# Delta rule and two-level mixture of experts on one core: loads and stores asked for in transfers by rows

## The chip, the core and the metric

The kernel runs on one core of a Trainium2 chip. The core has a matrix engine (TensorE, in the profile PE, its weight loads PEld), a vector engine (VectorE, DVE), a scalar engine (ScalarE, ACT), GpSimd (POOL) and SyncE (SP), which issues most of the DMAs; sixteen DMA engines move the bytes. The metric is the time of one execution on the device in microseconds (us). A difference is called faster or slower here when it is over 2%; smaller ones count as the same.

## The reference

The first half is a delta rule with a state per batch and head, B=4, H=8, S=768 tokens, D=48; the second sends each of the 3072 tokens to one of 16 experts, group first, then expert in the group.

```python
k_n = k / (np.linalg.norm(k, axis=-1, keepdims=True) + 1e-06)
for t in range(S):
    y[:, :, t] = einsum('bhd,bhde->bhe', q[:, :, t], state)
    v_old = einsum('bhde,bhd->bhe', state, k_n[:, :, t])
    state = state + beta_t * einsum('bhd,bhe->bhde', k_n[:, :, t], v[:, :, t] - v_old)
x = y.transpose(0, 2, 1, 3).reshape(3072, 384)
g_idx = argmax(x @ w_group);  e_idx = argmax(xg @ w_expert[g])        # one expert for a token
out[tok] = g_w * e_w * (np.maximum(x_tok @ w1[g, e], 0) @ w2[g, e])   # 384 -> 1024 -> 384
```

All is float32.

## The kernel before

**The recursion** works on 24 chunks u of 32 tokens, all four batches and eight heads at once. For each chunk there are two loads. `load_kq(u)` brings keys and queries as columns: 112 rows (48 rows of the even heads, 16 of padding, 48 of the odd heads) of 1024 numbers; with a second argument it brings one half (a = 0 the keys, a = 1 the queries), 112 rows of 512. `load_kv(u)` brings keys and values as rows, 128 of 832 numbers. Twelve buffers (`NB`) hold the first kind, three (`NV`) the second. `load_con(0)` and `load_con(1)` bring the constants in two parts, the second with the identity matrix.

`gram(u)` multiplies a chunk's keys with its keys and queries (L258 for the first two chunks, L273); `inverse(g)` builds for four chunks at once, by many small VectorE instructions (L313 to L416, most of them L382 and L388), the inverse that replaces the steps inside a chunk, and `spread` puts it into `mtb` (L425 on VectorE, L427 on ScalarE). `scale(u)` multiplies the chunk's values with a norm (`vh`, L463, VectorE); it is the first reader of `kv`. `advance(u)` is the step of the chain: the products with the state (L486, L495), with the inverse (L503), the update of the state (L514, which reads the keys in `kv`), the output (L528), and copies by ScalarE between them. `logits(u)` and `route(r)` choose experts and sort tokens while the recursion goes on.

**The prologue** runs the products of chunks 0 to 9 before the recursion's first step. The SP queue gets the loads in bursts: `begin(bursts[i])` puts, ahead of each load, a ScalarE copy of one column into the tile that is to be filled (L800), so the load waits in SP's queue until ScalarE has come past the products before it. All five engines run in the order in which the program is written, so an instruction that waits holds what stands behind it on its engine. Before the first L503 stand, on TensorE, the products of chunks 8 and 9 and four products that clear the state's memory (L834).

**In step u of the recursion** the program issues at the end `load_kq(u + 12)` (until chunk 23 is asked for), `load_kv(u + 3)`, the store of the chunk's output `x` to `x_dram` (L990), and from u = 12 on one of the `pieces` of the weights of the first expert: first six with two transfers of 32 rows each of its `w1` (L151), then four of its `w2` (L158). `scale(u + 2)` stands in the first half of step u, so `load_kv(u + 3)`, which has to wait until L514 has read the buffer, is wanted in the first half of the step behind it. SP's other work, the loads of later experts (L167 to L174) and the transfers of results (L1171 to L1176), comes behind the recursion.

**The experts** follow from about 220 us on: for each a load of 3 MB of weights, a gather of its tokens, two products (L1112, L1131), and a scatter.

## Time and profile before

| | before |
|---|---|
| time, median of 3 runs | 494.39 us (488.39 to 496.58) |
| profiled execution: time | 493.09 us |
| profiled execution: span | 491.1 us |
| busy PE / DVE / ACT / POOL | 450.0 / 240.6 / 192.8 / 176.8 us |
| mean rate of all DMAs | 198 GB/s |

The profile is one execution. Its span is the time from the program's first to its last instruction; 2.0 us of the time lie outside it. In rows of the timeline, the first two numbers are the start and the length in us, `SPq` is SP issuing a transfer (its length is that of the issue, not of the transfer), and brackets tell how long the engine stood idle before the instruction and what ended that. In the chain (work followed back from the end to what released it) a row `DMA` has the issue of a transfer and the time until its landing released the next. A table by windows has for each stretch the busy time of each engine with the count of instructions, then the TensorE clock granted, the mean share of the 16 DMA engines that was busy, and their rate in GB/s.

### The profile page before, as it was taken

How to read it: one execution, taken by the hardware profiler on the slowest of the kernel's cores; microseconds unless marked ns; L12 is line 12 of the kernel's file. 1: busy time of each engine (PE TensorE's matmuls, PEld its weight loads, DVE VectorE, ACT ScalarE, POOL GpSimd, SP SyncE). 2: the span in 40 equal slices, each digit the busy share in tenths (PEclk: the TensorE clock that was granted, in tenths of full speed). 3: DMA queues.
4: the chain of work that ended last, by engine and by line, in shares of the span. 5: the costliest groups of instructions: out<-in, count | busy, mean ns of one | idle time of the engine just before them, and what ended most of it. 6: DMA issues, size and time to landing. Idle time of an engine off the chain costs nothing.

```text
span 491.1 us, 18102 instructions
## 1 busy us (share of the span) xinstructions
PE 450.0 (92%) x7730; PEld 425.9 (87%) x7730; DVE 240.6 (49%) x872; ACT 192.8 (39%) x413; POOL 176.8 (36%) x300
## 2 busy tenths in 40 slices
PE   3338999999999999999999999999999999999992
PEld 3335888888888888789999999999999999999992
DVE  4988998997999998565201201220122112201110
ACT  3335579688897976541112111111211111111120
POOL 0031310415416400103456355544745456255131
PEclk9999599899999999999999999999999999999997
DMA  5566344455434455307977877858997789778820
GB/s 163 149 186 200 100 150 153 128 151 174 144 109 123 145 161 166 90 23 177 370 238 229 277 254 208 300 186 274 318 298 228 255 302 322 248 215 273 308 80 27
DMA packets 56757, 97.07 MB, mean 198 GB/s; under 512 B 18974, under 2 KB 41433, under 8 KB 56675
## 3 DMA queue, kind: packets, MB, share of 16 engines
q1 hardware_dynamic: 50755, 85.89, 54.6%
q0 software_dynamic: 5920, 10.00, 6.5%
q8 instruction: 62, 1.02, 0.9%
q14 instruction: 20, 0.16, 0.1%
HBM read 81.75 MB, written 14.27 MB: 196 GB/s over the span
## 4 chain that ended last, share of the span: by engine, by line
PE 55%; DMA 12%; issue 11%; ACT 7%; DVE 7%; POOL 7%; SPq 0%; POOLq 0%; DVEq 0%
PE y_ps L1131 16%; PE h_ps L1112 16%; DMA out_dram<-yo,to_i 7%; POOL xq L1084 5%; DMA kqt<-in_kq_dram 4%; PE w_ps L503 4%; PE s_ps L514 3%; ACT s_bd L520 3%; PE a_ps L486 2%; PE o_ps L528 2%; PE o_ps L495 2%; DVE m L388 2%; DVE below L382 2%; PE t_ps L554 2%; PE l_ps L456 1%
## 5 line engine op out<-in xcount | busy, mean ns | idle before, releaser
L1131 PE MATMUL y_ps<-hid,w 128*128 128x224 f32 (+15 forms) x768 | 132.2, 332 | 0.0
L1131 PEld LDWEIGHTS y_ps<-hid,w 128*128 128x128 f32 x768 | 129.1, 190 | 0.3
L1112 PE MATMUL h_ps<-xt,w 128*128 128x232 f32 (+14 forms) x720 | 122.7, 330 | 0.0
L1112 PEld LDWEIGHTS h_ps<-xt,w 128*128 128x128 f32 x720 | 120.1, 190 | 0.3
L1084 POOL DMA_INDIRECT xq<-x_dram,from_q x92 | 87.6, 952 | 35.0 <-issue 24.1
L1134 DVE COPY yt<-y_ps 128x232 f32<-128x232 f32 (+13 forms) x14 | 5.1, 365 | 144.4 <-PE y_ps L1131 144.4
L1115 ACT ACTIVATE hid<-h_ps 128x448 f32<-128x448 f32 (+15 forms) x64 | 32.1, 501 | 100.2 <-PE h_ps L1112 98.2
L1143 POOL DMA_INDIRECT out_dram<-yo,to_i x32 | 34.1, 1065 | 93.2 <-DVE yo L1181 83.7
L1136 ACT ACTIVATE yt<-y_ps 128x224 f32<-128x224 f32 (+15 forms) x34 | 11.4, 336 | 116.6 <-PE y_ps L1131 116.6
L382 DVE TENSOR_TENSOR below<-m 128x16 f32<-128x16 f32 (+4 forms) x180 | 53.3, 299 | 0.2
L388 DVE TENSOR_TENSOR m<-m,below 128x16 f32<-128x16 f32 (+4 forms) x180 | 53.0, 295 | 0.4
L520 ACT ACTIVATE s_bd<-s_ps 48x768 f32<-48x768 f32 x46 | 37.0, 804 | 5.6 <-PE s_ps L514 5.1
L1181 DVE TENSOR_SCALAR yo<-yr,gate 128x384 f32<-128x384 f32 (+14 forms) x28 | 11.1, 420 | 39.8 <-DMA yr<-y_dram 31.4
L503 PEld LDWEIGHTS w_ps<-f,mtb 64*64 64x64 f32 x736 | 24.6, 141 | 6.0 <-ACT f L490 3.9
L503 PE MATMUL w_ps<-f,mtb 64*64 64x48 f32 x736 | 27.5, 227 | 1.4 <-ACT f L490 1.4
L427 ACT ACTIVATE mtb<-mt,con 128x256 f32<-128x256 f32 x39 | 28.0, 741 | 0.0
L514 PE MATMUL s_ps<-w,kv 32*112 32x96 f32 x736 | 25.3, 273 | 0.9 <-ACT found L871 0.3
L514 PEld LDWEIGHTS s_ps<-w,kv 32*112 32x112 f32 x736 | 21.3, 178 | 3.8 <-ACT w L507 1.5
L528 PE MATMUL o_ps<-w,gqm 64*64 64x48 f32 x576 | 21.4, 225 | 2.5 <-issue 2.3
L486 PE MATMUL a_ps<-s_bd,kqt 112*32 112x96 f32 x736 | 21.1, 257 | 1.1 <-ACT s_bd L520 1.1
L495 PE MATMUL o_ps<-s_bd,kqt 112*32 112x96 f32 x736 | 21.8, 259 | 0.2 <-issue 0.2
L528 PEld LDWEIGHTS o_ps<-w,gqm 64*64 64x64 f32 x576 | 19.1, 139 | 3.3 <-issue 2.5
(184 smaller groups left out, 543.8 us busy)
## 6 DMA issues: line engine op xcount, KB each, us to landing
w<-in_w_dram SPq DMA_DIRECT2D x29, 1536.0 KB, 10.7
kv<-in_kv_dram SPq DMA_DIRECT2D x24, 416.0 KB, 3.2
kqt<-in_kq_dram SPq DMA_DIRECT2D x20, 448.0 KB, 4.8
x_dram<-x SPq DMA_DIRECT2D x24, 192.0 KB, 2.2
w<-in_w_dram SPq DMA_DIRECT2D x24, 128.0 KB, 3.8
y_dram<-yq SPq DMA_DIRECT2D x36, 84.0 KB, 9.4
yr<-y_dram SPq DMA_DIRECT2D x14, 192.0 KB, 2.5
kqt<-in_kq_dram SPq DMA_DIRECT2D x8, 224.0 KB, 3.6
```

The costliest lines, as they stand in the source:

```text
L382: nc.vector.tensor_tensor(t, column.to_broadcast(like), row.to_broadcast(like), op=ALU.mult)
L388: nc.vector.tensor_tensor(to, to, t, op=ALU.add)
L495: nc.tensor.matmul(o_ps[quads[b], 2 * j:2 * j + 2, :], lhsT=kqt[0:KR, 1, j, quads[b]], rhs=s_bd[0:KR, b, j], start=(j == 0), stop=False, s ...
L503: nc.tensor.matmul(w_ps[b, h], lhsT=mt[b, uu * H + (h % 2) * NP + h // 2], rhs=f[b, h], start=(h == 0), stop=True, skip_group_check=True)
L514: nc.tensor.matmul(s_at[0:KR, b, j], lhsT=k[quads[b], j, 0:KR], rhs=w[quads[b], 2 * j:2 * j + 2], start=(u == 0 and j == 0), stop=True, sk ...
L520: nc.scalar.activation(s_bd[rows, :, :, hh, :], s_at[rows, :, :, hh * D:(hh + 1) * D], ACT.Copy)
L528: nc.tensor.matmul(o_ps[b, h], lhsT=gq[b, hq].rearrange("p a t -> p (a t)"), rhs=w[b, h], start=(u == 0 and h == 0), stop=True, skip_group ...
L1084: nc.gpsimd.indirect_dma_start(out=xq[:, g, :], out_offset=None, in_=x_dram[:, :].rearrange("n (q c) -> (n q) c", q=4), in_offset=bass.Ind ...
L1112: nc.tensor.matmul(h_ps[:, k], lhsT=w1[:, j, (f + k) * 128:(f + k + 1) * 128], rhs=xt[:, j, 0:R], start=(j == 0), stop=(j == DC - 1), skip ...
L1115: nc.scalar.activation(hid[:, f:f + 2], h_ps, ACT.Relu)
L1131: nc.tensor.matmul(y_ps, lhsT=w2[:, f, j * 128:(j + 1) * 128], rhs=hid[:, f], start=(f == 0), stop=(f == FC - 1))
L1143: put = nc.gpsimd.indirect_dma_start(out=out[:, :], out_offset=bass.IndirectOffsetOnAxis(ap=to[0:P, i:i + 1], axis=0), in_=yo[0:P, :], in_ ...
```

## The change

A helper `by_rows` issues one transfer for each range of rows. Whole loads of keys and queries are cut into rows 0 to 31, 32 to 63 and 64 to 111; the loads of one half stay whole. Loads of keys and values, the second part of the constants and each of the four pieces of the first expert's `w2` become four transfers of 32 rows, and the store of `x` two of 64.

```diff
+    def by_rows(out, in_, cuts):
+
+        for a, b in zip(cuts, cuts[1:]):
+            nc.sync.dma_start(out=out[a:b], in_=in_[a:b])
+
+    quarters_of = range(0, 129, 32)
...
-            out.append(lambda a=a, b=b: nc.sync.dma_start(out=w2[:, a:b], in_=d[:, a:b]))
+            out.append(lambda a=a, b=b: by_rows(w2[:, a:b], d[:, a:b], quarters_of))
...
         def load_kq(u, a=None):
+            cuts = (0, 32, 64, KR) if a is None else (0, KR)
             half = slice(0, 2) if a is None else slice(a, a + 1)
-            nc.sync.dma_start(out=kqt_[u % NB][0:KR, half],
-                              in_=kq_d[u].rearrange("p (a j t) -> p a j t", a=2, j=NP)[:, half])
+            by_rows(kqt_[u % NB][0:KR, half],
+                    kq_d[u].rearrange("p (a j t) -> p a j t", a=2, j=NP)[:, half], cuts)

         def load_kv(u):
-            nc.sync.dma_start(out=kv_[u % NV], in_=kv_d[u])
+            by_rows(kv_[u % NV], kv_d[u], quarters_of)
...
-            nc.sync.dma_start(out=con[:, part], in_=const_d[:, part])
+            by_rows(con[:, part], const_d[:, part], quarters_of if i else (0, 128))
...
-                    nc.sync.dma_start(out=x_dram[1 + u * 128:1 + (u + 1) * 128], in_=xs[u])
+                    by_rows(x_dram[1 + u * 128:1 + (u + 1) * 128], xs[u], (0, 64, 128))
```

The order of the computing instructions is the same on PE, DVE, ACT and POOL; SP has 439 rows instead of 288, and waits for loads become waits for their parts. Three places show it.

SP, in the prologue: the burst behind the products of chunk 0 and the one behind it (kv_117 and kv_118 are the buffers of chunks 0 and 1, con is the second part of the constants, kqt_113 and kqt_114 are for chunks 8 and 9). Before:

```order
L204 DMA kv_117<-in_kv_dram 128x832 [waits DMAHW0_49,Activation_49]
L210 DMA con<-in_const_dram 128x753 [waits DMAHW1_49]
L204 DMA kv_118<-in_kv_dram 128x832 [waits DMAHW2_49]
L200 DMA kqt_113<-in_kq_dram 112x1024 [waits DMAHW3_49,Activation_49]
L200 DMA kqt_114<-in_kq_dram 112x1024 [waits DMAHW4_49,Activation_49]
```

After, its last ten of 18:

```order
L145 DMA kv_118<-in_kv_dram 32x832 [waits DMAHW0_49]
L145 DMA kv_118<-in_kv_dram 32x832 [waits DMAHW1_49]
L145 DMA kv_118<-in_kv_dram 32x832 [waits DMAHW2_49]
L145 DMA kv_118<-in_kv_dram 32x832 [waits DMAHW3_49]
L145 DMA kqt_113<-in_kq_dram 32x1024 [waits DMAHW4_49,Activation_49]
L145 DMA kqt_113<-in_kq_dram 32x1024 [waits DMAHW5_49]
L145 DMA kqt_113<-in_kq_dram 48x1024 [waits DMAHW6_49]
L145 DMA kqt_114<-in_kq_dram 32x1024 [waits DMAHW7_49,Activation_49]
L145 DMA kqt_114<-in_kq_dram 32x1024 [waits DMAHW0_49]
L145 DMA kqt_114<-in_kq_dram 48x1024 [waits DMAHW1_49]
```

Twelve issues instead of three now stand ahead of the loads for chunks 8 and 9, and the last of these wait for parts of the same burst: the transfer eight places ahead is a part of con or of kv_118.

SP, one step of the recursion (x is the chunk's output). Before:

```order
L200 DMA kqt_110<-in_kq_dram 112x1024 [waits DMAHW7_49,PE_49]
L204 DMA kv_119<-in_kv_dram 128x832 [waits DMAHW0_49,DVE_49,PE_49]
L990 DMA x_dram<-x_1941 128x384 [waits DMAHW1_49,Activation_49]
L200 DMA kqt_111<-in_kq_dram 112x1024 [waits DMAHW2_49,PE_49]
L204 DMA kv_117<-in_kv_dram 128x832 [waits DMAHW3_49,DVE_49,PE_49]
```

After:

```order
L145 DMA kqt_110<-in_kq_dram 32x1024 [waits DMAHW1_49,PE_49]
L145 DMA kqt_110<-in_kq_dram 32x1024 [waits DMAHW2_49]
L145 DMA kqt_110<-in_kq_dram 48x1024 [waits DMAHW3_49]
L145 DMA kv_119<-in_kv_dram 32x832 [waits DMAHW4_49,DVE_49,PE_49]
L145 DMA kv_119<-in_kv_dram 32x832 [waits DMAHW5_49,PE_49]
L145 DMA kv_119<-in_kv_dram 32x832 [waits DMAHW6_49,PE_49]
L145 DMA kv_119<-in_kv_dram 32x832 [waits DMAHW7_49,PE_49]
L145 DMA x_dram<-x_1999 64x384 [waits DMAHW0_49,Activation_49]
L145 DMA x_dram<-x_1999 64x384 [waits DMAHW1_49]
```

A step has nine transfers on SP instead of three, one more than there are counters, so the second half of x waits for the first part of the same step's kqt.

PE, a step of the recursion at chunk 4 (g_ps is the product of a later chunk's keys and queries, s_ps the state's update). Before:

```order
L273 MATMUL g_ps_1491<-kqt_106 32x64 [waits DMAHW3_49,Activation_49]
L273 MATMUL g_ps_1491<-kqt_106 32x64 x31
L514 MATMUL s_ps<-w_1487,kv_117 112x96 [waits DMAHW1_49,Activation_49]
L514 MATMUL s_ps<-w_1487,kv_117 112x96 x15
L456 MATMUL l_ps_1545<-wr,xt_1450 128x20 [waits PE_49,Activation_49]
```

After:

```order
L281 MATMUL g_ps_1537<-kqt_106 32x64 [waits DMAHW6_49,DMAHW5_49,Activation_49]
L281 MATMUL g_ps_1537<-kqt_106 32x64 [waits DMAHW7_49]
L281 MATMUL g_ps_1537<-kqt_106 32x64 x30
L522 MATMUL s_ps<-w_1533,kv_117 112x96 [waits Activation_49]
L522 MATMUL s_ps<-w_1533,kv_117 112x96 [waits DMAHW0_49]
L522 MATMUL s_ps<-w_1533,kv_117 112x96 [waits DMAHW1_49]
L522 MATMUL s_ps<-w_1533,kv_117 112x96 [waits DMAHW2_49]
L522 MATMUL s_ps<-w_1533,kv_117 112x96 x12
```

One wait for a load has become three or four, at the first products that read its rows; the second product of a g_ps already needs the last rows (the odd heads). VectorE's `vh` likewise waits for four counters instead of one.

## Prediction

> **What bounds the kernel now.** I read the table by windows first, to see which stretch a slower or faster load can touch.

> ```profile
> core 0: us, PE busy (x) PEld busy (x) DVE busy (x) ACT busy (x) POOL busy (x), PEclk, DMA share, GB/s
> 29.00:31.00 2.00, 0.00 (x0) 0.00 (x0) 2.00 (x7) 1.35 (x2) 0.00 (x0) 1.00 1.01 332
> 31.00:33.00 2.00, 0.00 (x0) 0.00 (x0) 2.00 (x7) 0.00 (x0) 1.69 (x7) 1.00 1.02 236
> 46.00:140.00 94.00, 90.59 (x2822) 80.31 (x2826) 87.50 (x348) 75.33 (x148) 25.86 (x82) 0.91 0.44 136
> 220.00:456.00 236.00, 236.00 (x1387) 235.35 (x1387) 42.62 (x87) 39.11 (x87) 117.63 (x132) 1.00 0.80 259
> 225.40:227.40 2.00, 2.00 (x13) 2.00 (x12) 1.50 (x8) 0.27 (x2) 1.57 (x2) 1.00 0.99 254
> ```

> From 220 us on TensorE is busy all of 236 us, and none of those transfers is edited: nearly half of the span cannot move. Between 46 and 140 us, most of the recursion, the DMA engines are busy 44% of the time; VectorE has 87.50 of 94 us of work, TensorE 90.59. There a load matters by when it lands, not by its bytes. Only the first 46 us have stretches where TensorE does nothing while the DMA engines are full (29 to 33 us). So I took the chain next, up to 41 us and around the one place behind that where it passes through a load.

> ```profile
> 6.79 4.30 DMA kqt<-in_kq_dram
> ...
> 13.40 4.67 DMA kqt<-in_kq_dram
> ...
> 20.39 2.58 DMA kqt<-in_kq_dram
> ...
> 28.30 6.21 DMA kqt<-in_kq_dram
> ...
> 35.81 1.09 PE g_ps L273 x59
> 36.89 2.86 PE s_ps L834 x4
> 39.76 1.64 PE w_ps L503 x32
> ...
> 78.79 3.96 DMA kv<-in_kv_dram
> 82.84 0.56 DVE vh L463
> ```

> Four loads of keys stand in the chain ahead of the first L503 at 39.76; the third (halves) is not cut by the change. The other three, 15.18 us, are what it can shorten or lengthen, and 78.79 is the one load of `kv` in the recursion that the chain goes through. The list of waits says how much VectorE lost to loads at all: two waits.

> ```profile
> DVE vh L463 <- DMA kv<-in_kv_dram: 3.7, 2, 2.3
> ```

> **The most that the prologue can give.** Behind the loads a second chain ends almost as late: the first inverse on VectorE.

> ```profile
> 28.29 0.56 DVE L463 TENSOR_TENSOR vh<-kv,normt 128x384 f32<-128x384 f32 x1 [1.43 <-DMA kv<-in_kv_dram]
> 36.18 0.47 DVE L425 TENSOR_SCALAR mtb<-mt,con 128x256 f32<-128x256 f32 x1
> 37.83 0.72 ACT L427 ACTIVATE mtb<-mt,con 128x256 f32<-128x256 f32 x1
> ```

> L425 ends at 36.65 and L427 takes 0.72, so L503 could start at 37.37 at the earliest: 39.76 - 37.37 = 2.39 us is the cap, and 3.82 if VectorE's own 1.43 us of waiting for the first `kv` went too.

> **Part 1, loads of the prologue.** What a part costs is its issue and its landing.

> ```profile
> 1.69 1.36 SPq L200 DMA_DIRECT2D kqt<-in_kq_dram  x3
> ...
> 24.56 0.35 SPq L204 DMA_DIRECT2D kv<-in_kv_dram  x1
> 24.95 1.21 SPq L210 DMA_DIRECT2D con<-in_const_dram  x1
> 26.22 0.42 SPq L204 DMA_DIRECT2D kv<-in_kv_dram  x1
> ...
> 167.40 2.31 SPq L151 DMA_DIRECT2D w<-in_w_dram  x2
> ```

> Three issues in 1.36 us are 0.45 us apart; two of 32 rows in 2.31 us show that it can be 1.16 each. No part of 96 to 192 KB of a load was seen alone; the nearest rows are L151, 32 rows and 128 KB, and the store of 192 KB, L990. The views by line tell their landings, and that of a whole `kv`, in the order L151, L990, L204:

> ```profile
> DMA to landing us min/median/max: 2.7/3.8/3.8
> DMA to landing us min/median/max: 1.8/2.2/3.2
> DMA to landing us min/median/max: 3.1/3.2/4.3
> ```

> At 13.40 the first load of the pair now ends with its third part, asked for at 13.40 + 2 x 0.45 = 14.30, landed 2.7 to 3.8 us later, at 17.0 to 18.1; before it was 18.07. I take 17.6, a gain of **0.5**. At 6.79 the same sum gives 10.4 to 11.5 against 11.09: **0**. For the pair at 28.30 SP is the question. Before, SP was done with what stands ahead at 26.64; now twelve issues from 24.56 on end at 24.56 + 12 x 0.45 = 29.96, 1.66 us behind the old 28.30. The first load's third part then goes at 30.86 and lands at 33.6 to 34.7; before, 28.30 + 6.21 = 34.51. The old landing was late since the engines were full (1.01 and 1.02 in 29 to 33 us) with the same bytes that they get now. I take 33.9, a gain of **0.6**; the bounds are a gain of 0.9 and a loss of 0.2. The two gains add up along the chain to 1.1, below the cap. They are hidden if L427 moves later by over 1.3 us (39.76 - 1.1 - 37.37).

> The first `kv` has its last part asked for at 24.56 + 1.35 = 25.91; by L990's landing it is there at 27.7 to 29.1, by L151's at 28.6 to 29.7, before just ahead of 28.29. I take 28.5, a loss of **0.2** on VectorE, which carries it into the stretch to 140 us. The constants of the second part are first read by TensorE at 36.89 (L834) and cost nothing: even two microseconds more are covered.

> **Part 2, the recursion.** `load_kq` is asked for twelve chunks ahead: nothing. `load_kv` is short of time only where VectorE is the bound.

> ```profile
> 71.32 0.33 SPq L204 DMA_DIRECT2D kv<-in_kv_dram  x1
> ...
> 74.87 0.56 DVE L463 TENSOR_TENSOR vh<-kv,normt 128x384 f32<-128x384 f32 x1
> ```

> There the load of 71.32 landed at about 74.5 (median 3.2) and had 0.3 us to spare; the one of 78.79 came 2.30 us late. With four parts the last is asked for 1.35 us later and is smaller than any row: landing 1.35 + 1.8 = 3.15 to 1.35 + 2.7 = 4.05 us after the first issue, against 3.2. I take 3.5, so 0.3 late at 82.84 and covered at 74.87: a loss of **0.3**, bounds a gain of 0.05 and a loss of 1.35 (0.85 at 82.84, 0.5 at 74.87). SP itself has room: nine issues of 0.45 are 4.1 us of a step of 7.47 (71.32 to 78.79), and the parts of one step come up when PE or ACT lets them.

> Stores of `x` in halves and `w2` in parts have no reader within 4 us: `x_dram` is read by gathers at the end of the recursion, the first expert's `w2` behind 220 us. They cost nothing as long as SP isn't late by a step.

> Added waits: three more on VectorE before each `vh`, one more on ScalarE before `x`, four or five on TensorE a step.

> ```profile
> L463 DVEq EVENT_SEMAPHORE  x15: 21/21/21, 42.2 to 190.2; - x15
> ```

> One takes 21 ns, and fifteen of them stood ahead of `vh`, while VectorE waited there for loads at two places only: the others were passed under the instruction before. I take **0**; if none were hidden, 8 x 24 x 0.021 = 4.0 us over all engines, of which perhaps half in the chain.

> **Sum.** -0.5 + 0 - 0.6 + 0.2 + 0.3 = -0.6 us. The profiled execution's time is 493.09, its span 491.1; so 492.5. The median of the runs shown is 1.3 us above the profiled one and the runs lie 8.2 us apart, so this is no change that can be measured: under 2% (9.9 us) I call it the same.

> **A rule against the change.** The row that bears on it stands above: in 225.4 to 227.4 us, with parts of 32 rows of the second expert's `w1` in flight beside a gather, the engines were 99% busy at 254 GB/s; in 29 to 31 us, with whole loads, 101% at 332. So parts of 32 rows may move at 254/332 = 0.77 of the rate. *Rival A* is that:

> ```profile
> kv<-in_kv_dram SPq DMA_DIRECT2D x24, 416.0 KB, 3.2
> kqt<-in_kq_dram SPq DMA_DIRECT2D x20, 448.0 KB, 4.8
> ```

> By these sizes a `kv`, 0.426 MB, takes 1.68 us instead of 1.28, so it lands 0.4 later still, and the first load of a pair, 0.459 MB, 1.81 instead of 1.38. Three pairs by 0.4 and two tight `kv` by 0.4 are 2.0, with the sum 494.5. Against it speaks 31 to 33 us, 236 GB/s with whole loads of 112 rows. [...]

> **Rival B, slower: the counters.** With eight counters a part waits for the part eight places ahead. Parts 0.45 us apart hold SP up once they need over 8 x 0.45 = 3.6 us to land. In the burst of 24.56, 18 parts would go in 2.25 rounds; at the 6.21 us of the row of 28.30 that is 14.0, so the last lands at 38.5 instead of 35.8 (the second product starts at 35.81), 2.7 us later than before. Loads of `kv` that meet a slow issue (1.16 instead of 0.45 us) are 2.1 us later; two such at tight places and the 0.3 make 4.5. In all 493.1 + 2.7 + 4.5 = **500.3**. For it speaks that the issue of con took 1.21 us; against it that a whole load in the recursion lands in 3.2, a part hardly above 3.6.

> **Rival C, faster: parts land earlier everywhere.** If parts spread evenly over the engines and the first ones start sooner, the prologue gives its cap of 3.82 and the `kv` of 78.79 its 2.30: 493.1 - 6.1 = **487.0**. The chain's long landings, 6.21 against 4.30 for the same bytes, show that there is room; against it, 2.30 us at that place come from a load that was asked for late (78.79, by L514), and parts cannot be asked for sooner.

> **That it does nothing** is the forecast's near neighbour, 493.1, and inside its own range.

> **How the numbers follow.** Forecast with its own range 490.5 to 494.0: 0.47. Rival A, 494.5: 0.18. B, 500.3: 0.13. C, 487.0: 0.18. Something else: 0.04. The range goes from C to short of B's time, with the loss of 2 to 4 us from waits that aren't hidden inside: 487 to 500. Over 2% against 494.39 is below 484.5 or above 504.3; no case lies there. For tails of C and of B and the rest I leave 0.03 and 0.04; within 2%, 0.93.

> **What would show it.** Right: the pair of 28.30 still asked for by SP at about 30 us, its first load landed at 33.5 to 34.7, first L503 near 38.7; `vh` waiting for loads in total 3 to 5 us; 220 us and behind shifted as a whole, with the same length. Part 1 is wrong if TensorE's waits for `kqt` don't fall or SP's issues in the prologue lie over 0.5 us apart; part 2 if `vh` waits at more than three places; the waits were not free if TensorE's step grows where no load is late. The forecast is off most if a clock below 1.00 (0.91 on the mean of 46 to 140 us) falls elsewhere in the changed run, since that moves TensorE by more than all terms here.

## The result, and the profile after

| | before | after |
|---|---|---|
| median, on one chip, 22 runs each | 492.31 us (487.98 to 498.48) | 494.24 us (490.82 to 499.2) |
| profiled execution: time / span | 493.09 / 491.1 us | 495.46 / 493.7 us |
| ratio after to before | | 1.0071, 95% interval 1.0047 to 1.0095 |

The change makes the kernel slower by 0.7%, 3.5 us. That is under the 2% that counts as a difference here, but the interval leaves no doubt of its sign, and the forecast had the other sign: 0.6 us faster. (Ratios compare undisturbed runs alone, so they can differ a little from the ratio of two medians.)

The table by windows shows where the DMA engines lost work. The rows answer to those of before: PE, PEld, DVE, ACT and POOL busy, the clock, the engines' share and GB/s.

```profile
29.00:31.00 2.00, 0.00 (x0) 0.00 (x0) 1.72 (x3) 1.65 (x3) 0.00 (x0) 1.00 0.73 198
31.00:33.00 2.00, 0.00 (x0) 0.00 (x0) 2.00 (x9) 0.00 (x0) 0.70 (x2) 1.00 0.61 177
33.00:35.00 2.00, 0.00 (x0) 0.00 (x0) 1.86 (x5) 0.00 (x0) 1.78 (x9) 1.00 1.01 272
46.00:140.00 94.00, 88.81 (x2874) 78.28 (x2873) 91.28 (x372) 77.34 (x151) 32.35 (x82) 0.96 0.53 145
220.00:456.00 236.00, 235.81 (x1439) 234.47 (x1438) 44.59 (x96) 39.26 (x88) 117.58 (x132) 1.00 0.81 260
```

From 220 us on nothing changed: TensorE is busy 235.81 of 236 us, before 236.00. The loss is ahead of that. In 29 to 33 us, where whole loads kept the engines 101% and 102% busy, they are now 73% and 61% busy, and from 30.9 to 31.8 us only 35%, at 87 GB/s. I read that as too little having been asked for; the chain says who did not ask. A row `SPq L145` is one issue of a part.

```profile
7.52 0.24 SPq L145
7.81 1.25 SPq L145
9.10 3.13 DMA kqt<-in_kq_dram
...
14.48 0.24 SPq L145
...
15.23 3.33 DMA kqt<-in_kq_dram
...
24.84 0.31 SPq L145
25.21 1.24 SPq L145
26.50 0.41 SPq L145
...
29.76 1.11 SPq L145
...
31.90 0.36 SPq L145
32.31 0.42 SPq L145
32.77 3.21 DMA kqt<-in_kq_dram
36.03 1.18 PE begin L281 x60
...
38.32 0.23 SPq L145
...
40.93 4.40 DMA kv<-in_kv_dram
45.41 0.56 DVE vh L471
```

Before, the chain went from ScalarE's copies straight to a DMA. Now SP stands in it almost without a gap from 24.84 to 32.77. Its timeline in groups, and the issues of these groups by length (min/median/max in ns, line L145 in 24 to 32 us):

```profile
24.84 2.54 SPq L145 DMA_DIRECT2D kv<-in_kv_dram  x4
27.43 1.82 SPq L145 DMA_DIRECT2D con<-in_const_dram  x4
29.30 2.51 SPq L145 DMA_DIRECT2D kv<-in_kv_dram  x4
31.90 7.59 SPq L145 DMA_DIRECT2D kqt<-in_kq_dram  x9
```

```profile
L145 SPq DMA_DIRECT2D kv<-in_kv_dram x8: 311/421/1243, 24.8 to 31.4; - x8
L145 SPq DMA_DIRECT2D con<-in_const_dram x4: 419/422/429, 27.4 to 28.8; - x4
```

Twelve issues took 7.0 us (24.84 to 31.81); the three of before took 2.1 (24.56 to 26.64). Most of them lie 0.46 us apart, two took 1.24 and 1.11 us. So the keys of chunk 8 were asked for from 31.90 on, before at 28.30, and landed at 32.77 + 3.21 = 35.98, before at 34.51. Behind chunk 8's product come three parts of chunk 10's keys, and only then the four parts of the **third kv**, that of chunk 2. Its last part is issued at 40.93; before, one issue brought it all:

```profile
37.29 0.38 SPq L204 DMA_DIRECT2D kv<-in_kv_dram  x1
...
42.23 0.56 DVE L463 TENSOR_TENSOR vh<-kv,normt 128x384 f32<-128x384 f32 x1 [0.45 <-PE g_ps L273]
```

```profile
45.41 0.56 DVE L471 TENSOR_TENSOR vh<-kv,normt 128x384 f32<-128x384 f32 x1 [2.68 <-DMA kv<-in_kv_dram]
```

The third `vh` starts 3.18 us later. Of these, 0.5 would have been left without the wait of 2.68 us for `kv`, since GpSimd, whose norms VectorE needs first, started 0.99 us later than before: it reads the second constants (32.30 instead of 31.31). VectorE is the bound for the next hundred microseconds (it is busy for 91.28 of the 94 us from 46 to 140, before 87.50), so it can carry a delay on.

This pair of profiles doesn't show that it did. From 46 to 115 us VectorE of before lost 5.9 us to waits, 2.3 for the `kv` of 78.79 and 3.6 for GpSimd, that of after only 2.0, and the twelfth `vh` starts at 115.19 in before and at 114.25 in after. The granted clock (the third number from the end) also fell at different places, in before at 46 to 60 us, in after at 205 to 212:

```profile
46.00:60.00 14.00, 13.78 (x310) 12.28 (x310) 13.93 (x58) 8.98 (x17) 3.27 (x12) 0.56 0.31 99
```

```profile
205.00:212.00 7.00, 6.14 (x134) 5.20 (x135) 1.53 (x8) 3.27 (x6) 1.26 (x2) 0.76 0.32 80
```

The 2.5 us by which the first product of the experts is later (222.86 instead of 220.38) arise in the second of these rows; ahead of it, at the L503 before the last, after is still 0.27 us early (199.78 instead of 200.05). So what the late `vh` is worth has to be read from the other kernels below. The waits of `vh` for loads in total:

```profile
DVE vh L471 <- DMA kv<-in_kv_dram: 4.4, 2, 2.7
```

A second, smaller loss stands later, where TensorE and ScalarE bound the step. The first L503 (now L511) of two steps behind each other, and ScalarE's wait for the update of the state in one of them, before and after:

```profile
167.98 1.14 PE L503 MATMUL w_ps<-f,mtb 64*64 64x48 f32 x32
174.03 1.20 PE L503 MATMUL w_ps<-f,mtb 64*64 64x48 f32 x32
...
170.82 1.62 ACT L520 ACTIVATE s_bd<-s_ps 48x768 f32<-48x768 f32 x2 [0.32 <-PE s_ps L514]
```

```profile
167.41 1.13 PE L511 MATMUL w_ps<-f,mtb 64*64 64x48 f32 x32
173.55 1.13 PE L511 MATMUL w_ps<-f,mtb 64*64 64x48 f32 x32
...
170.34 1.62 ACT L528 ACTIVATE s_bd<-s_ps 48x768 f32<-48x768 f32 x2 [0.40 <-PE s_ps L522]
```

The step is 6.14 us instead of 6.05, at a clock of 1.00 in both, and ScalarE waits 0.08 us longer for the product that reads `kv`.

### The profile page after: what moved, and what is told of

Same layout as the page of the kernel before. It is cut to its first block, busy times and chain, and to the rows that moved or that the text cites. A ratio compares the mean times of both kernels' runs of the same rounds, so it can differ in the third digit from the quotient of the medians.

```text
span 493.7 us, 18341 instructions
## 1 busy us (share of the span) xinstructions
PE 451.8 (92%) x7730; PEld 425.1 (86%) x7730; DVE 240.1 (49%) x872; ACT 192.9 (39%) x413; POOL 183.1 (37%) x300
## 3 DMA queue, kind: packets, MB, share of 16 engines
q8 instruction: 62, 1.02, 0.9%
## 4 chain that ended last, share of the span: by engine, by line
PE 61%; DMA 15%; ACT 7%; DVE 4%; issue 4%; SPq 3%; POOL 3%; DVEq 0%; POOLq 0%; ACTq 0%
PE y_ps L1139 19%; PE h_ps L1120 19%; DMA out_dram<-yo,to_i 6%; PE w_ps L511 4%; DMA kqt<-in_kq_dram 3%; PE a_ps L494 3%; PE o_ps L536 3%; DMA y_dram<-yq 3%; PE o_ps L503 3%; PE s_ps L522 3%; SPq L145 3%; ACT s_bd L528 2%; DMA yr<-y_dram 2%; PE l_ps L464 2%; PE t_ps L562 2%
## 5 line engine op out<-in xcount | busy, mean ns | idle before, releaser
L511 PEld LDWEIGHTS w_ps<-f,mtb 64*64 64x64 f32 x736 | 23.2, 135 | 5.4 <-ACT f L498 3.4
L511 PE MATMUL w_ps<-f,mtb 64*64 64x48 f32 x736 | 26.1, 220 | 1.1 <-ACT f L498 0.9
L522 PE MATMUL s_ps<-w,kv 32*112 32x96 f32 x736 | 24.3, 267 | 1.1 <-ACT found L879 0.3
L494 PE MATMUL a_ps<-s_bd,kqt 112*32 112x96 f32 x736 | 22.6, 264 | 2.1 <-ACT s_bd L528 1.9
L281 PE MATMUL begin<-kqt 48*32 48x32 f32 (+1 forms) x512 | 9.8, 277 | 14.5 <-DMA kqt<-in_kq_dram 10.1
L281 PE MATMUL g_ps<-kqt 48*32 48x64 f32 (+1 forms) x1152 | 18.0, 236 | 5.6 <-DMA kqt<-in_kq_dram 3.6
L503 PE MATMUL o_ps<-s_bd,kqt 112*32 112x96 f32 x736 | 22.6, 261 | 0.4 <-issue 0.3
```

What stands on the lines that cost most here:

```text
L494: nc.tensor.matmul(a_ps[quads[b], 2 * j:2 * j + 2, :], lhsT=kqt[0:KR, 0, j, quads[b]], rhs=s_bd[0:KR, b, j], start=False, stop=True, skip_ ...
L503: nc.tensor.matmul(o_ps[quads[b], 2 * j:2 * j + 2, :], lhsT=kqt[0:KR, 1, j, quads[b]], rhs=s_bd[0:KR, b, j], start=(j == 0), stop=False, s ...
L511: nc.tensor.matmul(w_ps[b, h], lhsT=mt[b, uu * H + (h % 2) * NP + h // 2], rhs=f[b, h], start=(h == 0), stop=True, skip_group_check=True)
L522: nc.tensor.matmul(s_at[0:KR, b, j], lhsT=k[quads[b], j, 0:KR], rhs=w[quads[b], 2 * j:2 * j + 2], start=(u == 0 and j == 0), stop=True, sk ...
```

## The experiments

All were timed beside runs of before on the same chip. "K" stands for the theory that the third `vh` sets the time. Some expectations speak of an equal clock: spans of one kernel fall by 4.0 us per 0.01 of mean granted clock (one slope through all runs, a level for each kernel and chip), and the difference of two levels is meant.

| kernel | third `vh` at | twentieth `vh` at | ratio to before | 95% interval | us over before at an equal clock |
|---|---|---|---|---|---|
| before | 42.23 | 172.53 | 1 | | |
| after | 45.41 | 171.76 | 1.0071 | 1.0047 to 1.0095 | |
| e10 nothing cut | 41.78 | 169.01 | 0.9995 | 0.9957 to 1.0034 | 0.6 |
| e7 second weights alone | 41.15 | 168.43 | 1.0003 | 0.9963 to 1.0044 | -0.7 |
| e2 loads of the recursion alone | 40.84 | 167.65 | 1.0031 | 0.9982 to 1.0081 | 0.3 |
| e18 after, prologue whole | 41.20 | 169.65 | 1.0029 | 0.9999 to 1.0059 | 1.1 |
| e19 the same, stores of x whole | 41.78 | 168.83 | 1.0036 | 1.0004 to 1.0068 | 0.9 |
| e14 keys of the prologue alone | 44.69 | 170.40 | 1.0046 | 1.0010 to 1.0083 | 1.6 |
| e1 prologue alone | 45.76 | 171.78 | 1.0047 | 0.9994 to 1.0100 | 3.4 |
| e15 kv and constants of the prologue alone | 47.24 | 172.91 | 1.0083 | 1.0045 to 1.0121 | 3.1 |
| e17 prologue in halves | 46.17 | 172.82 | 1.0080 | 1.0048 to 1.0111 | 2.4 |
| e12 after, stores of x whole | 46.26 | 172.32 | 1.0115 | 1.0075 to 1.0154 | 4.3 |
| e3 stores of x and second weights alone | 41.30 | 169.80 | 1.0117 | 1.0044 to 1.0190 | 2.7 |
| e6 stores of x alone, by rows | 41.69 | 169.31 | 1.0153 | 1.0078 to 1.0229 | 2.9 |
| e11 stores of x alone, by columns | 41.92 | 168.78 | 1.0119 | 1.0055 to 1.0184 | 2.7 |
| e16 small second store | 41.48 | 165.95 | 1.0044 | 1.0001 to 1.0088 | 0.8 |
| e4 constants and second kv late | 45.25 | 171.69 | 1.0121 | 1.0076 to 1.0165 | 2.8 |
| e9 third kv early | 42.28 | 167.10 | 1.0013 | 0.9967 to 1.0059 | 0.3 |
| e8 after, prologue's kv whole, third kv ahead | 42.78 | 173.26 | 1.0047 | 1.0000 to 1.0094 | 2.3 |
| e13 the same, stores of x whole | 42.04 | 173.44 | 1.0113 | 1.0054 to 1.0172 | 2.8 |

The twentieth `vh` stands near the end of the stretch in which VectorE is the bound. Leaving out before, whose waits are told above, it lies at 165.95 to 169.80 in the kernels with a whole prologue and its order untouched and in e9, and at 170.40 to 173.44 in all others. The kernels of the second group are 1.6 to 4.3 us slower at an equal clock (after has no such figure), those of the first -0.7 to 1.1 us, but for the three with whole loads and the stores of x in halves (2.7 to 2.9). So a late VectorE goes with a longer time. No row shows the way from there to the end: the last `vh` starts at 190.35 to 198.21 with the prologue whole and at 195.35 to 198.79 with it in parts, the first product of the experts at 212.24 to 222.31 and at 217.58 to 222.86. That link rests on the times alone.

### Which part of the change it is

e1 leaves all loads and stores whole but those of the prologue, e2 all but the recursion's, e3 all but the stores of x and the second weights. Against after:

```diff
 e1: only u <= 12 of the keys, u < 3 of kv, and the constants are cut
-            by_rows(kv_[u % NV], kv_d[u], quarters_of)
+            by_rows(kv_[u % NV], kv_d[u], quarters_of if u < NV else (0, 128))
 e2: the other way round; constants, x and w2 whole
 e3: keys, kv and constants whole; x in (0, 64, 128), w2 in quarters_of
```

> Only the loads of the prologue are cut (keys and queries of chunks 4 to 12, keys and values of chunks 0 to 2, the second constants); the loop's loads, the stores of x and the pieces of w2 are whole. Theory P (SP's pace: issues 0.46 us apart, some 1.1 to 1.25, put the loads of chunks 8 and 9 and of the third kv behind twelve or more issues): 1.004 to 1.008 of the time before, the loads for chunk 8 first asked for at 31 to 32 us instead of 28.3, TensorE's first L503 1 to 2.5 us later, VectorE waiting 2 to 3 us for the third kv. Theory R (loads of kv in the loop land too late for VectorE): 1.000 to 1.002. Theory W (added waits and counters in the loop): 1.000.

> Only the loads asked for in the loop are cut (keys and queries of chunks 13 to 23, keys and values of chunks 3 to 23). Theory P: 0.999 to 1.001, first L503 where it was before. Theory R: 1.004 to 1.008, with VectorE waiting for kv at three or more places between 55 and 110 us. Theory W: 1.002 to 1.006 without such waits, TensorE's steps longer.

> Only the stores of x are cut in two and the pieces of the first expert's w2 in four. Theory P and theory R: 0.999 to 1.001. Theory W: 1.000 to 1.003, through ScalarE's wait for two counters before x and SP's longer work in a step.

Medians: e1 496.78, e2 494.00, e3 496.01 us, before 493.35. e1 costs 3.4 us at an equal clock and has its third `vh` at 45.76, like after. e2 measured 1.0031: no gap at `vh` beyond those of a whole prologue, but the late steps at 6.14 us. e3, expected to be free, measured 1.0117 from six runs, with an interval that is wide. Taken apart in e6 and e7:

```diff
 e6 against before
-                    nc.sync.dma_start(out=x_dram[1 + u * 128:1 + (u + 1) * 128], in_=xs[u])
+                    by_rows(x_dram[1 + u * 128:1 + (u + 1) * 128], xs[u], (0, 64, 128))
 e7 against before: each piece of w2 by_rows(..., quarters_of)
```

> Before with one edit: the stores of x in two transfers of 64 rows each, nothing else cut. Theory K (the time follows the start of the third chunk's work on VectorE, that is when the kv of chunk 2 has landed; in the traces so far that vh started at 42.23 in before, 45.41 in after, 45.76 with the prologue cut, 45.25 with constants and second kv asked for late, 40.84 and 41.30 in the two kernels that leave the prologue whole): third vh at 41 to 42.3 as in before, ratio 0.997 to 1.003. Rival S (stores and second weights are the cost: the kernel with only these two cut measured 1.0117 of before, from six runs): if the stores carry it, 1.006 to 1.012 and SyncE or the engines visibly late by a step between 110 and 220 us.

> Before with one edit: each piece of the second weights of the first experts in four transfers of 32 rows, nothing else cut. Theory K: third vh at 41 to 42.3, ratio 0.997 to 1.003, with at most the end of the recursion (160 to 220 us) or the first expert different. Rival S, if the second weights carry it: 1.006 to 1.012, with TensorE waiting for weights of the first expert or SyncE late between 150 and 220 us. If this and the stores alone both stay under 1.004, the 1.0117 was the spread of six runs.

e7: 493.15 us against 492.12, free as forecast. e6: 497.86 us. So the stores carry it, and next it was tried whether that is the rows:

```diff
 e11 against before
+                    for cols_of_x in (slice(0, H * D // 2), slice(H * D // 2, H * D)):
+                        nc.sync.dma_start(out=x_dram[1 + u * 128:1 + (u + 1) * 128, cols_of_x],
+                                          in_=xs[u][:, cols_of_x])
 e16 against before: x whole, and behind it
+                    nc.sync.dma_start(out=spare[u:u + 1], in_=xs[u][0:1, 0:128])
 e10 against before: all through by_rows, nothing cut
```

> Nothing is cut: the loads and stores go through the new helper, each as one transfer, so every engine has the instructions of before. It shows what a program that only is built and loaded anew is worth. Theories K and S both say 0.997 to 1.003. If it lies at 1.005 or above, differences of that size between two kernels (the stores of x in halves at 1.0153, before with late constants at 1.0121) can't be put down to their edits.

> Before with the stores of x in two transfers by columns, each over all 128 rows and 192 of 384 columns; nothing else cut. As many issues, and as many transfers that come between the loads, as with halves by rows, which measured 1.0153 from six runs. Theory S1 (a second store each step costs by its issue, and by what it holds up behind it): 1.005 to 1.015, TensorE's idle time without a releaser 6 to 8 us between 40 and 222 us as with halves by rows (7.5) instead of 3 to 4. Theory S2 (rows 0 to 63 alone are what costs): 0.998 to 1.003. If neither halves by rows nor by columns cost anything, both stay at 1.000.

> Before with the stores of x whole and one more store in each step behind it: the first row of x, 128 columns, 512 bytes, into DRAM that nothing reads. It adds the issue and the wait of the second half of x, without its bytes or its packets. Theory I (the second issue of a step is what costs: 1.0117, 1.0153 and 1.0119 with halves by rows or columns): 1.006 to 1.014. Theory B (two larger transfers side by side, or their packets, cost): 0.998 to 1.003.

e10 measured 492.24 us against 491.48, ratio 0.9995: a program built anew is worth nothing. e11: 498.77 us, so halves by columns cost as much as by rows, and it isn't the rows. e16: 490.48 us against 487.65, 1.0044 (1.0001 to 1.0088), between the two theories. TensorE's idle time without a releaser, on which S1 leaned, was 7.0 us in e11, but 8.5 in e10, which is as fast as before: it shows nothing. What a second store of x costs in these kernels is left open below.

### Whether the third kv is what counts

e4 and e9 cut nothing and move transfers.

```diff
 e4 against before
-            2 * RG: [(kv_[0], [lambda: load_kv(0), lambda: load_con(1), lambda: load_kv(1)])],
-            2 * RG + 2: [of_kq(2 * RG), of_kq(2 * RG + 1)],
+            2 * RG: [(kv_[0], [lambda: load_kv(0)])],
+            2 * RG + 2: [of_kq(2 * RG), of_kq(2 * RG + 1),
+                         (kv_[1], [lambda: load_con(1), lambda: load_kv(1)])],
 e9 against before
-        after_gram = {2 * RG: [of_kq(2 * RG + 2), (kv_[2], [lambda: load_kv(2)])],
+        after_gram = {2 * RG: [of_kq(2 * RG + 2)],
-            2 * RG + 2: [of_kq(2 * RG), of_kq(2 * RG + 1)],
+            2 * RG + 2: [of_kq(2 * RG), of_kq(2 * RG + 1), (kv_[2], [lambda: load_kv(2)])],
```

> No load is cut; the second constants and the keys and values of chunk 1 are asked for behind the loads of chunks 8 and 9 instead of ahead of them. If what stands ahead of the loads of chunks 8 and 9 on SP's queue and in the DMA engines sets when TensorE goes on (theory P's place): 0.994 to 0.998, those loads landed at 32 to 33.5 us instead of 34.5 and 35.6, first L503 1 to 2 us earlier. If VectorE's first inverse sets it: 0.999 to 1.001. If the constants, now late, hold L834: 1.002 or more.

> Before, nothing cut, with one transfer moved forward: the kv of chunk 2 is asked for right behind the keys of chunks 8 and 9 (about 29 us) instead of behind chunk 8's Gram product (37.29). Theory K: it lands by 37, third vh starts when VectorE is free, 40.5 to 41.8 instead of 42.23, so 0.4 to 1.5 us gained; ratio 0.996 to 1.000. Rival (the engines' load in 29 to 35 us sets the pace): chunk 9's keys land 1.3 us later, and the ratio is 1.000 to 1.004.

e4 was meant to gain and lost: 497.62 us against 493.35, 1.0121 (1.0076 to 1.0165). VectorE's third `vh` stood at 45.25 (up to there at a clock of 1.00), the same place as in after, with nothing cut at all. That made K, but it wasn't a `kv` that held it: the second `vh` started at 37.36 (before 37.23), and then VectorE waited for GpSimd, which had waited for the late constants until 36.16 (before 31.31).

```profile
36.16 0.63 POOL L829 COPY what<-con 128x48 f32<-128x48 f32 x1 [22.38 <-DMA con<-in_const_dram]
42.49 0.35 DVE L358 RECIPROCAL r<-nrm 128x32 f32<-128x32 f32 x1 [4.58 <-POOL nrm L343]
```

So e4 speaks for a wider form of K, that a late VectorE costs time whatever makes it late, and it shows a second load that VectorE hangs on by way of GpSimd. TensorE wasn't held (first L503 at 39.49, before 39.69).

e9 gave 491.87 us against 492.12, 1.0013 (0.9967 to 1.0059): asking for the third `kv` at 28.28 instead of 37.29 moved the third `vh` to 42.28, not ahead of before, since VectorE then waited for TensorE. K had expected a gain; the ratio lies where the rival put it, with chunk 9's product 0.6 us later (36.32 instead of 35.72).

```profile
42.28 0.56 DVE L471 TENSOR_TENSOR vh<-kv,normt 128x384 f32<-128x384 f32 x1 [2.39 <-PE w_ps L511]
```

Early, it was worth nothing in this one kernel. e14 and e15 cut the two kinds of loads of the prologue apart, e17 all of them in halves.

```diff
 e14 against before: load_kq
+            cuts = (0, 32, 64, KR) if a is None and u <= NB else (0, KR)
 e15 against before: load_kv, and load_con as in after
+            by_rows(kv_[u % NV], kv_d[u], quarters_of if u < NV else (0, 128))
 e17: as e1, with (0, 64, KR) for keys and (0, 64, 128) for kv and constants
```

> Before with only the keys of the prologue (chunks 1 to 12) in three parts; kv, constants, stores and the recursion whole. The forecast on record gained 0.5 and 0.6 us from just these. Theory K: chunk 8's keys are still asked for at 28.3, the last part at 29.2, landed near 34.0 (before 34.5); behind them the three parts of chunk 10's keys put the kv of chunk 2 off by 0.9, so the third vh starts at 42 to 43 (before 42.23, after 45.41): ratio 0.998 to 1.003. Rival Q (parts of keys land later than whole loads, or keep TensorE waiting for chunks 9 to 12): third vh at 44 or later or TensorE's waits for keys between 36 and 48 us over 3 us, ratio 1.004 to 1.008.

> Before with only the first three kv and the second part of the constants in four parts; keys, stores and the recursion whole. The forecast on record put 0.2 us on this. Theory K: SyncE is done with the twelve issues from 24.6 at about 31.5 instead of 26.6, chunk 8's keys are asked for at 31.6 to 31.9 instead of 28.3 and land at 35.5 to 36.5, the last part of the third kv is asked for at 39 to 39.7 (before 37.29), and the third vh starts at 43.5 to 44.8: ratio 1.004 to 1.008, most of what the whole prologue cost. Rival Q: the ratio stays at 0.998 to 1.003 and the keys carry the loss.

> The loads of the prologue in two parts of rows instead of three or four (keys 64 and 48, kv and constants 64 and 64); nothing else cut. Theory K: six issues stand from 24.6 on instead of twelve, done at about 28.3 to 29 (before 26.6, after 31.8), chunk 8's keys asked for at 28.5 to 29.5, third vh at 42.5 to 44: ratio 1.000 to 1.005, between before and the whole prologue in parts (1.0047 on this measure, 3.4 us at an equal clock). Rival (the loss is the size of a part, not the number of issues): with halves no loss at all, third vh at 41 to 42.3, ratio 0.997 to 1.000.

Medians 489.57, 492.15 and 491.24 us against 487.65. The timeline of SP in e15, then the third `vh` in e14, e15 and e17:

```profile
25.21 2.79 SPq L145 DMA_DIRECT2D kv<-in_kv_dram  x4
28.05 2.91 SPq L145 DMA_DIRECT2D con<-in_const_dram  x4
31.00 1.81 SPq L145 DMA_DIRECT2D kv<-in_kv_dram  x4
32.91 6.89 SPq L145 DMA_DIRECT2D kqt<-in_kq_dram  x3
39.90 1.94 SPq L145 DMA_DIRECT2D kv<-in_kv_dram  x4
```

```profile
44.69 0.56 DVE L471 TENSOR_TENSOR vh<-kv,normt 128x384 f32<-128x384 f32 x1 [3.41 <-DMA kv<-in_kv_dram]
```

```profile
47.24 0.56 DVE L471 TENSOR_TENSOR vh<-kv,normt 128x384 f32<-128x384 f32 x1 [3.92 <-PE o_ps L536]
```

```profile
46.17 0.56 DVE L471 TENSOR_TENSOR vh<-kv,normt 128x384 f32<-128x384 f32 x1 [3.27 <-DMA kv<-in_kv_dram]
```

The parts of `kv` and constants cost most when cut alone (1.0083), as K says: SP busy from 25.21 to 32.81, chunk 8's keys asked for at 32.91, while the engines were 60% and 54% busy at 29 to 33 us. The third `vh` came later than K's 43.5 to 44.8. But the parts of keys lose as well, 1.0046, where the forecast had its gains; there rival Q was right in place and ratio. The two sum to more than e1's 1.0047; the intervals are too wide to say why. And halves, six issues instead of twelve, cost no less than quarters: K's scaling with the number of issues failed, the expected 1.000 to 1.005 was 1.0080. In e17 the third `kv` was asked for in full at 39.98 and took 6.07 us to land. (In the row of e15, L536 stands as releaser; its chain goes through the DMA of `kv`, issued at 41.42 and there at 47.03.)

What the number of issues leaves out is the rate of the engines. Before, and then after, while the third `kv` is on its way:

```profile
39.00:41.00 2.00, 2.00 (x26) 1.31 (x26) 1.90 (x8) 0.00 (x0) 0.13 (x1) 1.00 1.03 342
41.00:43.00 2.00, 2.00 (x108) 1.84 (x106) 1.55 (x11) 1.52 (x4) 0.02 (x1) 1.00 1.07 293
```

```profile
41.00:43.00 2.00, 2.00 (x20) 0.98 (x20) 1.70 (x9) 0.00 (x0) 0.16 (x1) 1.00 1.04 229
43.00:45.00 2.00, 2.00 (x96) 1.84 (x96) 0.00 (x0) 0.97 (x3) 0.00 (x0) 1.00 1.00 227
45.00:47.00 2.00, 1.77 (x63) 1.55 (x56) 1.59 (x10) 1.90 (x5) 0.00 (x0) 1.00 1.08 228
```

Full engines moved 227 to 229 GB/s with keys in parts among their loads, instead of 293 and 342. It is the same elsewhere: 242 to 334 GB/s at 39 to 43 us in the other nine kernels with a whole prologue and its order untouched, 261 to 290 at 41 to 47 us in e15, where keys are whole, but 199 to 241 there in e1, e12 and e17 (303, 209 and 240 in e14). In e17 the engines were 95 to 103% busy at 235 to 240 GB/s already from 29 to 35 us, so halves lost by the rate more than by SP, whose six issues took 4.0 us. Both show at the third `kv`: with a whole prologue it was asked for at 35.80 to 37.19 and `vh` started 4.6 to 5.1 us behind that (the seven kernels in which `vh` waited for it), in the six with parts at 38.34 to 40.08 and 5.8 to 7.3 us behind. What each is worth isn't shown, since no kernel adds issues to the prologue without parts.

Over ten kernels with a whole prologue and its order untouched (before, e2, e3, e6, e7, e10, e11, e16, e18, e19) the third `vh` lies at 40.84 to 42.23, over six with the prologue in parts (after, e1, e12, e14, e15, e17) at 44.69 to 47.24. No trace falls between.

### What is left when the prologue is whole

e8 and e13 left the prologue's `kv` and constants whole, and put the third `kv` ahead of chunk 10's keys; e13 has the stores of x whole too.

```diff
 e8 against after (e13: x in (0, 128) besides)
-            by_rows(kv_[u % NV], kv_d[u], quarters_of)
+            by_rows(kv_[u % NV], kv_d[u], quarters_of if u >= NV else (0, 128))
-            by_rows(con[:, part], const_d[:, part], quarters_of if i else (0, 128))
+            by_rows(con[:, part], const_d[:, part], (0, 128))
-        after_gram = {2 * RG: [of_kq(2 * RG + 2), (kv_[2], [lambda: load_kv(2)])],
+        after_gram = {2 * RG: [(kv_[2], [lambda: load_kv(2)]), of_kq(2 * RG + 2)],
```

> After with three things undone in the prologue: the first three kv and the second part of the constants are whole again, and the kv of chunk 2 is asked for ahead of the three parts of chunk 10's keys. Keys in three parts everywhere, kv of the recursion in four, stores and second weights cut as in after. Theory K: SyncE is done with the burst from 24.6 at about 26.6, chunk 8's keys are asked for at about 28.3 and landed at 34.0 to 34.6, the kv of chunk 2 is asked for at about 36 and landed near 41, third vh at 41 to 42 instead of 45.4; the ratio falls from 1.007 to 0.996 to 1.003. Rival S: nothing of that matters, the ratio stays at 1.006 to 1.012. Rival W (added waits in the recursion): third vh early, but each step of the recursion longer, ratio 1.004 to 1.008.

> The kernel of the second call with kv and constants of the prologue whole and the third kv ahead of chunk 10's keys (1.0047), and the stores of x whole too. Keys are in three parts, kv of the recursion and second weights in four. Theory L: both lanes are as early as in before, third vh at 41.5 to 43, ratio 0.997 to 1.003. If the cut loads of the recursion cost by their added waits: TensorE's steps late in the recursion 6.14 instead of 6.06 us as in the three kernels that cut them, and the ratio 1.001 to 1.004.

e8: 495.60 us against 492.12, 1.0047 (1.0000 to 1.0094). e13: 499.32 us against 491.48, 1.0113 (1.0054 to 1.0172). Their third `vh` stood at 42.78 and 42.04, and they did not come back: the third `vh` alone doesn't set the time. Rows of TensorE in e13 show the place:

```profile
42.71 0.27 PE L281 MATMUL g_ps<-kqt 48*32 48x64 f32 x2 [1.85 <-DMA kqt<-in_kq_dram]
44.61 0.84 PE L281 MATMUL g_ps<-kqt 48*32 48x64 f32 x62 [1.63 <-DMA kqt<-in_kq_dram]
```

The keys that were put behind the third `kv` now keep TensorE waiting for 3.5 us. VectorE became late behind the third `vh`: at the fourth it waited 2.14 (e8) and 0.77 us (e13) for `kv`, at the eighth 1.57 us for `kv` (e8) and 3.46 us for ScalarE (e13), so that their twentieth `vh` is the latest of all. That edit mixed two things and can't tell them apart, so e18 and e19 left the order alone. e12 is after with the stores whole.

```diff
 e12 against after
-                    by_rows(x_dram[1 + u * 128:1 + (u + 1) * 128], xs[u], (0, 64, 128))
+                    by_rows(x_dram[1 + u * 128:1 + (u + 1) * 128], xs[u], (0, 128))
 e18 against after: keys cut only for u > NB, kv only for u >= NV, constants whole
 e19: e18 with x whole
```

> After with the stores of x whole again, all else cut as in after. Theory L (two lanes: the prologue's late kv delays VectorE's by 3 to 3.5 us, the stores in halves delay TensorE's by about as much, and the later of the two sets the end): third vh at 45.2 to 45.8 as in after, ratio 1.005 to 1.009, no better than after. If the two add up: ratio 0.995 to 1.002. If the stores were the whole loss: 0.998 to 1.002.

> After with all loads of the prologue whole, in the old order: keys of chunks 1 to 12, first three kv and constants. The recursion's loads, the stores of x and the second weights are cut as in after. Third vh at 40.8 to 42.3 as in the kernels with a whole prologue. Theory D (the prologue is the whole loss of the change as it stands; the stores in halves cost nothing beside cut loads): 0.998 to 1.004. Theory X (the stores in halves cost by themselves, hidden in after behind the late prologue): 1.006 to 1.014.

> The same with the stores of x whole too, so that only the recursion's loads of keys and kv and the second weights are cut. Both theories: 0.998 to 1.004, TensorE's late steps 6.14 instead of 6.06 us. Above 1.006 the cut loads of the recursion cost more than the 1.0031 that they measured alone, and that would explain why the kernel with whole kv, constants and stores stayed at 1.0113.

e12 496.65 us against 491.48; e18 489.50 and e19 489.17 us against 487.70. With the prologue whole, all that the rest of the change costs is 1.0029 and 1.0036, and e2 had 1.0031: three kernels with cut loads in the recursion agree on 0.3%, some 1.5 us (at an equal clock 0.3 to 1.1 us; only the interval of e19 leaves out 1). Their steps late in the recursion are 6.13 to 6.14 us, as in all seven that cut `kv` there (after, e2, e8, e12, e13, e18, e19), and 6.06 in those that don't; 24 steps of 0.08 us would be 1.9 us, by estimate, so the added waits can be all of it. The stores of x in halves cost nothing beside cut loads: 1.0029 with them, 1.0036 without, and after without them (e12) is no faster: 1.0115, above theory L's 1.005 to 1.009 and far from the sum of two losses. Theory X falls with this.

**What adds up:** e1's 0.47% for the prologue and the 0.3% of the recursion give 0.8%, and after measured 0.71%. This agrees but proves little: e1's interval reaches from 0.9994 to 1.0100, and e12, with the same two parts, measured 1.15%.

**What stays open:** with whole loads, a second store of x costs 1.2 to 1.5% (e3, e6, e11), beside cut loads nothing; a small one (e16) cost 0.4%. No row of these traces carries it; ScalarE's wait instruction ahead of `x` took 38 instead of 17 ns in 20 steps, 0.4 us in all. These three kernels have six runs each, and in e6 and e11 the clock was lower (0.978 and 0.979 on the mean) than in before (0.985); at an equal clock 2.7 to 2.9 us are left. No version measured here beats before.

## Why the forecast was wrong

The time of after, 494.24 us, lies in the range, 1.7 us above the forecast, and within 2% it is the same; but the sum said -0.6 and the ratio of the runs says +3.5. That the time lies in the range is luck, as the range reached from 487 to 500. By its steps:

- **"Twelve issues from 24.56 on end at 24.56 + 12 x 0.45 = 29.96."** This step failed. The start and the pitch were nearly right (24.84, 0.46), but two issues took 1.24 and 1.11 us, and the end was 31.81. The row of 1.21 us for con in the profile of before was used for rival B and left out of the sum.
- **"I take 33.9, a gain of 0.6."** The keys landed at 35.98. Asked for in parts they took 4.08 us from the first issue to the last landing instead of 6.21, but they were asked for 3.6 us later. The argument "with the same bytes that they get now" took for granted that the engines would be full as before; in after they were 73% and 61% busy at 29 to 33 us.
- **The third kv was not in the sum.** It stands behind chunk 8's product and chunk 10's keys, so seven issues instead of two came before its landing. The sum went by the chain of waits, in which it didn't appear before, as VectorE's 0.45 us of waiting there were for TensorE. This is the step that moved most: 3.18 us at the third `vh`, where the "cap" of the prologue had been sought at the first L503 (39.76, now 42.03). (The chain of before also has a fifth load of keys, at 1.69; it is of one half, so not cut, and the sum stands.)
- **The constants "cost nothing: even two microseconds more are covered".** That holds for TensorE (L834), but GpSimd reads them first, at 31.31, and VectorE waited 1.09 us for GpSimd already in before. In after they made GpSimd 0.99 us later; behind the wait for the third `kv` that doesn't show in the time. In e4, with the constants later still, it was 4.58 us of waiting.
- **The pairs at 6.79 and 13.40**, forecast at 0 and -0.5: the first was asked for at 7.52 instead of 6.79, since the load ahead of it was late, and took 4.71 us until 9.10 + 3.13 = 12.23, instead of 4.30, with one issue of 1.25 us in it. The second, asked for later by that (14.48 instead of 13.40), took 4.08 instead of 4.67 us: the gain of 0.5 was there, but it landed at 18.56, before at 18.07.
- **The first kv, +0.2:** `vh` started at 29.28 instead of 28.29, with 1.74 us of waiting instead of 1.43. Right in sign, 0.1 above in wait; the rest is the later start.
- **The kv of 78.79, +0.3:** that wait is gone; the eighth `vh` starts at 85.17 instead of 82.84 and finds the load. With a late prologue it is covered, so the term was void. The total of 4.4 us for `vh` lies in the forecast's 3 to 5 by luck: it was lost at the first and third `kv`, not at the first and this one. In e18 and e2, where the prologue is whole, the waits of `vh` in the recursion weren't longer either.
- **Added waits, 0:** wrong, but small: 0.08 us a step where TensorE and ScalarE bound it, by row 0.32 to 0.40. The bound of 4.0 us held it; I took the value by VectorE's waits alone.
- **Stores of x and second weights, 0:** right for the weights (e7), right for the stores in the company of cut loads (e18 against e19), not in a kernel with whole loads.
- **The part behind 220 us:** right; from the first product of the experts to the end it is 270.7 us in before and 270.8 in after.

Of the rivals, A (a lower rate of parts) came closest, with 494.5 us, and its mechanism shows: at 33 to 35 us the full engines still moved 272 GB/s with parts in flight, but from 41 to 47 us, with the third `kv` among the loads, 228 on the mean, against 317 from 39 to 43 in before, a factor of 0.72 where A had taken 0.77. Its price, five loads by 0.4 us, isn't shown by itself. B (counters) had the right engine with the wrong reason: SP was late by the length and number of its issues, and its list of waits names ScalarE, TensorE and no counter. e17, in halves, came to 1.0080 with engines that were 95 to 103% busy from 29 to 35 us; in after they stood partly idle for the first four of these microseconds (73% and 61% busy), and SP was late.

## What to carry to other kernels

Here a transfer in parts cost an issue for each part, one behind the other on SP (twelve in 7.0 us instead of three in 2.1), and what paid most was not that transfer but the ones behind it in the queue (chunk 8's keys were asked for 3.6 us later): count the issues ahead of each load that something waits for, and use the longest issue in the profile beside the median (in after 1.24 us beside 0.42). Look at the rate of full engines too, which here fell with keys in parts from 317 to 228 GB/s where it counted. Then look at loads that land just in time, not only at those in the chain of before, and at what hangs on a load by way of another engine; the third `kv` came in time in before, and 0.8 to 1.5 us late in some kernels with a whole prologue (e10, e18, e3). In the recursion, where SP still waited for TensorE and ScalarE in 70.6 of 182 us (40 to 222 us), parts cost 0.3% (e2, e18, e19), and still each part brought a wait to its readers (late steps of 6.13 to 6.14 instead of 6.06 us).

## What the runs showed that I had not expected

- Issues at a pitch of 0.46 us and, in most bursts, one or two of 1.1 to 1.5 us among them (after 1.24 and 1.11, e15 1.50 twice, none in e16); the profile names nothing that they wait for.
- A load landing later can go with a later end though 400 us follow: 3.2 to 4.0 us at the third `vh` (after, e1, e12, against before) came with ratios of 1.0047 to 1.0115, 2.3 to 5.7 us.
- Single profiled executions lie as far apart as the whole effect: e10, which has the instructions of before, has a span of 493.6 us against 491.1, e16 one of 482.9 on another chip. Of such a trace only the place of a wait can be used, not its end.
